# The last 64 queries of a head pair: score products in quarters of TensorE

## Chip, cores and metric

The kernel runs on one core of a Trainium2 chip. The metric is the device time of one execution in microseconds. The kernel before takes 1059.11 us (median of 3 runs, 1058.5 to 1061.32).

## What is computed

Three layers follow one another on 4 batches of 576 tokens: an attention whose probabilities are cut off below the row's maximum less tau, a dense layer with a gate, and a layer of eight experts of which each token uses one. Only the first part of the attention is touched by the change:

```python
def _attn_ref(q, k, v, tau):            # q, k, v: 4 batches, 8 heads, 576 rows, 64 columns
    scale = 1.0 / np.sqrt(q.shape[-1])
    scores = scale * np.matmul(q, k.transpose(0, 1, 3, 2))
    thresh = np.max(scores, axis=-1, keepdims=True) - tau
    scores = np.where(scores >= thresh, scores, -1000000000.0)
    scores = scores - np.max(scores, axis=-1, keepdims=True)
    attn = np.exp(scores)
    attn = attn / (np.sum(attn, axis=-1, keepdims=True) + 1e-09)
    return np.matmul(attn, v)
# then x = attention's rows; g = h * sigmoid(h) with h = x @ w_in; x = g @ w_out;
# then each row through its best expert: gate * relu(x @ w1[e]) @ w2[e]
```

## The kernel before

The attention goes over 16 pairs of heads (4 batches, 4 pairs each). The two heads of a pair lie on the two halves of the 128 partitions: `o.k` has 128 partitions (64 for each head) and 576 columns, `o.q` has 640 columns. The first 512 columns of `o.q` are four chunks of 128 queries. The 64 queries that are left of each head share one chunk, the fifth (`ch == 4`): in its 128 columns the first head's queries stand in columns 0 to 63 of its own 64 partitions, the second head's in columns 64 to 127 of its own, and the host (`layout`) puts zeros elsewhere. One product over all 128 partitions then gives the scores of both heads, the first head's in partitions 0 to 63 of the bank, the second's in 64 to 127.

`score_pe` (L496 and after, the products at L513) makes the scores of a chunk. For chunks 0 to 3 the two heads are two products of 64 rows by 128 columns, in the upper and the lower half of TensorE, into two places of PSUM. The 576 keys are cut: for the first eight pairs (steps below `WIDE`, 72) into four pieces of 144 columns, so that two sets of scores fit side by side, and later into two pieces of 288. Behind the scores come, for each head of a chunk, the maximum on VectorE (`score_max`, L519), the threshold and the exponential on ScalarE (L522, L525), the mask on VectorE (`score_mask`, L540; for chunk 4 it writes `Pm`), transposes on TensorE (L577 and L585, for chunk 4 L593 and L597), copies out of PSUM (L295 on ScalarE, L297 on VectorE), and the products with the values (`values`, L669). Of those the last piece (`j == 4`) has 64 rows for each head:

```python
            for h in range(2):
                rows = slice(None) if j < 4 else HALF[h]
                k = 4 if j == 4 else 5 * h + j
                nc.tensor.matmul(
                    w.av[HALF[h], :nq], lhsT=st.o.vn[rows, k, :], rhs=st.pts[part][rows, k, :],
                    start=(j == 0), stop=(j == 4),
                )
```

Products of the dense layer (L709, L743) are mixed into the attention's from the end of the first batch on. What of them does not fit there, and all of the rest, runs behind the attention (L1117, L1369, L1928, L1932).

The order of the instructions on each engine is written by a planner before the kernel runs. `attend` (L885 and after, the scores' task at L904) makes a task for each step with an engine, an estimated duration, what it waits for and a rank. The planner plays the tasks through and takes, on each engine, the task of the lowest rank among those that can start first or at most its slack later. A TensorE task whose mode (scores, values, or none) differs from the last one's starts `SWITCH`, 0.1 us, later in this play. The score task of a chunk has 1.18 us, whichever chunk it is, rank `s - 0.6`; the maximum has rank `s - 1`, the exponential and the mask `s - 2`, where `s` counts the steps of all pairs. On the chip semaphores alone hold the instructions back; the plan sets their order, not their times.

Of the kernel before, what the change touches and what calls it, by code (L numbers as in the profile page):

```python
# [64 lines left out]
HALF = [slice(0, 64), slice(64, 128)]  # L65
# [195 lines left out]
class Kernel:  # L261
# [234 lines left out]
    def score_pe(self, st, ch, ws, uses):  # L496

        nc = self.nc
        for h, (w, use) in enumerate(zip(ws, uses)):
            w.nm = f"{ch}{h}" + st.nm  # L500
            bank = 3 if use.tag[0] == "B" else 0
            if use.wide:
                at = 512 * bank + 4 * APART * use.slot
                w.S = self.flat[:, at:at + 4 * APART].rearrange("p (a x) -> p a x", x=APART)[:, :, :PIECE]
            else:
                w.S = self.banks[:, bank:bank + 2, :288]
        lhsT = st.o.q[:, 128 * ch:128 * ch + 128]
        n, c = w.S.shape[1:]
        for a in range(n):
            for h, w in enumerate(ws):  # L510

                rows = HALF[h] if ch < 4 else slice(None)
                nc.tensor.matmul(  # L513
                    w.S[:, a], lhsT=lhsT[rows], rhs=st.o.k[rows, c * a:c * a + c], start=True, stop=True
                )

    def score_max(self, w):
# [367 lines left out]
    def attend(self, plan, pair, n, o, x_there):  # L885

        steps = self.steps(pair, o)
        st = steps[0][0]
# [4 lines left out]
        for a, step in enumerate(steps):  # L893
            s = 9.0 * n + a
            _, ch, h = step
            if h == 0:

                pe = []
                for i in range(2 if ch < 4 else 1):
                    w = Obj()  # L900
                    w.use = Token(f"{'AB'[i]}{(9 * n // 2 + n % 2 + (a + 1) // 2) % 2 if s < WIDE else 0}")
                    w.use.wide = s < WIDE
                    pe.append(w)
                score = plan.task(  # L904
                    "pe", 1.18, partial(self.score_pe, st, ch, pe, [w.use for w in pe]),
                    o.there + self.last_s + ([] if s < WIDE else self.last_wide),
                    tuple(w.use for w in pe), (o.k_use, o.q_use), rank=s - 0.6, slack=0.1, mode="scores",
                )
                self.last_s = [score]
                for x in (int(s) - 1, int(s)):  # L910
                    if x in self.held:
                        plan.link(score, self.held.pop(x))
            w = pe[h]
            scores, t = w.use, score
            use = [scores, Token("m"), Token("e")]
            if ch < 4 and h == 0 or ch == 4:
                p_use[ch] = Token("P" if ch < 4 else "Pm")
            mx = plan.task("dve", 0.67, partial(self.score_max, w), (t,), (use[1],), rank=s - 1, slack=0.3)
            t = plan.task("act", 0.84, partial(self.score_exp, w), (mx,), (use[2],), rank=s - 2, slack=0)
            mask = masks[ch, h] = plan.task(  # L920
                "dve", 0.81, partial(self.score_mask, step, w), [t] + list(masks.values())[-1:],
                ((p_use[ch],) if h == 0 else ()) + ((l_use,) if a == 0 else ()), use + [self.more_banks[x] for x in ("wide", "narrow")[s >= WIDE:]], rank=s - 2,
                slack=0.1,
            )
            if s < WIDE:
                self.last_wide = [mask]
            part = min(ch // 2, 1)
            for i, (tag, turn, pieces) in enumerate(self.turns(step)):
                if n == B * H // 2 - 1 and ch > 2:
                    tag = "M"  # L930
                tok = Token(tag)
                give = [self.more_banks["T"]] if tag == "T" else []
                if i and ch < 4:
                    after, us, used = [masks[x, y] for x in (ch - 1, ch) for y in range(2)], 0.24, [p_use[ch - 1], p_use[ch]]
                else:
                    after, us, used = [mask], 0.46 if ch < 4 else 0.3, [p_use[ch]]
                t = plan.task("pe", us, partial(turn, tok), after + (begun[part:part + 1] if i else []), (tok,), used, rank=s + -0.5, slack=0.1)
                for cols, move in pieces:
                    take = ()
                    if part not in part_use:  # L940
                        part_use[part] = Token(f"p{2 * part}")
                        take = (part_use[part],)
                    us = {512: (0.48, 0.6), 256: (0.26, 0.335), 64: (0.11, 0.13)}[cols]
                    x = plan.task(
                        "act", us[0], move, [t] + begun[part:part + 1], take, [tok] + give, rank=s, alt=("dve", us[1])
                    )
                    if take:
                        begun.append(x)
                    moved[part].append(x)
            if ch == 1 and h == 1 or ch == 4:  # L950
                tok = Token("M")
                us, mms, move = self.values(st, part, tok)
                t = plan.task(
                    "pe", 5 * us, partial(run_all, mms), moved[part] + o.v_there + av[-1:],
                    (tok,) if part else (tok, t_use), (part_use[part], o.v_use), rank=s + 1, mode="values",
                )
                av.append(t)
                moved["x"] = moved.get("x", []) + [
                    plan.task("act", 0.31, move, (t,), give=(tok,), rank=s, alt=("dve", 0.36))
                ]  # L960
        s = 9.0 * n + DEN
        dve, pe, act, store, load, mul, out = self.denominators(st)
# [1116 lines left out]
```

## Time and profile before

| | |
|---|---|
| median of 3 runs | 1059.11 us |
| the profiled execution | 1061.68 us |
| its span, first to last instruction | 1059.8 us |
| TensorE busy (matmuls) | 974.7 us, 92% |
| VectorE, ScalarE, GpSimd busy | 709.1, 542.3, 433.4 us |
| mean granted clock of TensorE | 0.965 of 2.4 GHz |

The page gives busy times over the whole span, and then digits for 40 slices of 26.5 us each. Matmuls are pipelined, so one that is listed with 0.29 us may be followed by the next after 0.12 us: the time that a group of matmuls takes is read from its start to the start of the next group, not from the durations. The clock that the profile calls PEclk is the share of 2.4 GHz that TensorE was granted; 0.5 is 1.2 GHz.

### The profile page before, as it was taken

Reading aid. Unit: us, or ns where it says so; the run is one execution under the profiler, and the core shown is the slowest. Engines: PE = TensorE matmul, PEld = TensorE weight load, DVE = VectorE, ACT = ScalarE, POOL = GpSimd, SP = SyncE. Lnnn points to the kernel's source line nnn. Section 1 sums busy time; section 2 is a strip of 40 time slices with the busy share of each in tenths; the row PEclk is TensorE's granted clock in tenths of the full one; section 3 lists DMA queues with packets and bytes.
Section 4 is the critical chain, followed back from the end, with each engine's and each line's share of the span. In section 5 each row is a group of like instructions: output and inputs, shape, how many; then the busy total and the mean of one; then the engine's idle time right before and its main releaser. Section 6 shows DMA issues by size and latency. Waiting matters only on the chain.

```text
span 1059.8 us, 18921 instructions
## 1 busy us (share of the span) xinstructions
PE 974.7 (92%) x6667; PEld 819.9 (77%) x6667; DVE 709.1 (67%) x1674; ACT 542.3 (51%) x1284; POOL 433.4 (41%) x444
## 2 busy tenths in 40 slices
PE   4878888999999999979999999999895999999995
PEld 4555566667667677868898898899784999999994
DVE  5778778877787676488588888888563435445521
ACT  4777766756676465466633333333443444444510
POOL 3565521334352120189645454444534444343210
PEclk7899999999999999999999999999896999999998
DMA  3234312334442221533532111111547555545400
GB/s 129 99 122 132 107 41 87 123 127 150 136 147 87 66 65 53 197 130 116 184 127 66 46 62 51 61 61 42 168 136 198 167 167 156 175 161 175 139 33 15
DMA packets 76401, 119.31 MB, mean 113 GB/s; under 512 B 11668, under 2 KB 38596, under 8 KB 76305
## 3 DMA queue, kind: packets, MB, share of 16 engines
q1 hardware_dynamic: 71857, 107.68, 31.6%
q0 software_dynamic: 4448, 10.40, 3.1%
q8 instruction: 53, 0.87, 0.3%
q14 instruction: 43, 0.35, 0.1%
HBM read 94.04 MB, written 24.82 MB: 112 GB/s over the span
## 4 chain that ended last, share of the span: by engine, by line
PE 40%; issue 6%; POOL 4%; DMA 3%; DVE 1%; ACT 1%; SPq 1%; another core or an unknown queue 0%; POOLq 0%; ACTq 0%; DVEq 0%
PE banks L1117 19%; PE banks L1369 11%; PE banks L1932 6%; PE banks L1928 2%; DMA xg<-x,idx 1%; POOL workwrt L351 1%; POOL workwrt L348 1%; POOL workwrt L352 1%; PE banks L1869 1%; POOL out L1955 1%; PE banks L1979 1%; DMA whrows<-part 1%; DMA idx<-table 0%; DMA when<-moe_expert_emb 0%; DMA part<-po 0%
## 5 line engine op out<-in xcount | busy, mean ns | idle before, releaser
L519 DVE TENSOR_REDUCE m<-banks 128x1 f32<-128x576 f32 x144 | 105.3, 752 | 41.0 <-PE banks L513 34.7
L1094 ACT ACTIVATE whe<-rawe 128x512 fp32r<-128x512 f32 x128 | 77.2, 625 | 92.8 <-PE banks L1932 28.1
L1098 DVE TENSOR_TENSOR wle<-rawe,whe 128x512 fp32r<-128x512 f32 x92 | 63.4, 714 | 88.6 <-ACT whe L1094 88.0
L540 DVE SCALAR_TENSOR_TENSOR P<-banks,m,e 128x576 f32<-128x576 f32 x128 | 103.5, 815 | 27.2 <-ACT e L525 14.4
L525 ACT ACTIVATE e<-banks,m 128x576 f32<-128x576 f32 x144 | 105.5, 733 | 13.4 <-PE banks L513 9.6
L513 PE MATMUL banks<-k,q 64*128 64x144 f32 (+3 forms) x792 | 98.5, 355 | 12.1 <-DVE m L519 4.4
L295 ACT ACTIVATE p<-banks 128x512 f32<-128x512 f32 (+2 forms) x166 | 76.2, 480 | 60.4 <-PE banks L577 49.7
L577 PE MATMUL banks<-ident,P 128*128 128x128 f32 x512 | 84.5, 290 | 19.1 <-ACT p L295 12.6
L577 PEld LDWEIGHTS banks<-ident,P 128*128 128x128 f32 x512 | 58.2, 145 | 47.8 <-ACT p L295 18.4
L669 PE MATMUL banks<-p,v 128*64 128x256 f32 (+3 forms) x640 | 93.6, 430 | 0.0
L513 PEld LDWEIGHTS banks<-k,q 64*128 64x128 f32 (+1 forms) x792 | 69.3, 196 | 28.1 <-issue 6.2
L1337 ACT ACTIVATE t<-banks 128x256 f32<-128x256 f32 x108 | 41.1, 380 | 96.9 <-PE banks L1117 95.3
L1098 POOL TENSOR_TENSOR wle<-rawe,whe 128x512 fp32r<-128x512 f32 x36 | 46.5, 1294 | 98.4 <-ACT whe L1094 78.7
L669 PEld LDWEIGHTS banks<-p,v 128*64 128x64 f32 (+1 forms) x640 | 41.7, 141 | 44.2 <-issue 24.6
L1342 DVE SCALAR_TENSOR_TENSOR g<-t,banks 128x256 f32<-128x256 f32 x108 | 45.0, 417 | 43.8 <-ACT t L1337 38.5
L522 ACT ACTIVATE m<-m,ntau 128x1 f32<-128x1 f32 x144 | 41.9, 291 | 41.0 <-DVE m L519 39.7
L1117 PE MATMUL banks<-xs_6h,wh 128*128 128x256 f32 x216 | 61.8, 286 | 0.0
L1117 PE MATMUL banks<-xs_6h,wl 128*128 128x256 f32 x216 | 61.5, 285 | 0.0
L1117 PE MATMUL banks<-xs_6l,wh 128*128 128x256 f32 x216 | 61.4, 284 | 0.0
L348 POOL TENSOR_TENSOR wa<-wa,wr 128x512 int32<-128x512 int32 x22 | 28.1, 1278 | 63.7 <-DVE wa L343 46.5
L1955 POOL DMA_INDIRECT out<-yr,idx x25 | 25.2, 1007 | 52.1 <-DVE yr L1967 39.2
L709 PE MATMUL banks<-xh,whi 128*128 128x256 f32 x144 | 43.8, 304 | 0.8 <-ACT p L295 0.8
(572 smaller groups left out, 3113.1 us busy)
## 6 DMA issues: line engine op xcount, KB each, us to landing
rawe<-moe_w SPq DMA_DIRECT2D x64, 512.0 KB
wraw<-moe_w_in SPq DMA_DIRECT2D x12, 512.0 KB
wraw<-moe_w_out SPq DMA_DIRECT2D x10, 512.0 KB
q<-q SPq DMA_DIRECT2D x15, 320.0 KB
v<-v SPq DMA_DIRECT2D x16, 288.0 KB
x_dram<-t SPq DMA_DIRECT2D x16, 288.0 KB
part<-po SPq DMA_DIRECT2D x18, 256.0 KB
xc<-x_dram SPq DMA_DIRECT2D x18, 256.0 KB
```

The costliest lines, as they stand in the source:

```text
L295: self.nc.scalar.activation(out=out, in_=src, func=AF.Copy)
L513: nc.tensor.matmul(w.S[:, a], lhsT=lhsT[rows], rhs=st.o.k[rows, c * a:c * a + c], start=True, stop=True)
L519: self.nc.vector.tensor_reduce(out=w.m[:, 0:1], in_=w.S, axis=AX.XY, op=ALU.max, negate=True)
L525: self.nc.scalar.activation(out=w.e, in_=w.S, func=AF.Exp, bias=w.m[:, 0:1])
L540: self.nc.vector.scalar_tensor_tensor(out=P.rearrange("p (a x) -> p a x", a=w.S.shape[1]), in0=w.S, scalar=w.m[:, 1:2], in1=w.e, op0=ALU.i ...
L577: nc.tensor.transpose(T[:, 128 * j:128 * j + 128], st.P[ch][:, c:c + 128], self.ident)
L669: nc.tensor.matmul(w.av[HALF[h], :nq], lhsT=st.o.vn[rows, k, :], rhs=st.pts[part][rows, k, :], start=(j == 0), stop=(j == 4),)
L1094: self.nc.scalar.activation(out=o.tiles[0][:, 2 * a:2 * a + 2], in_=o.raw[:, 2 * a:2 * a + 2], func=AF.Copy)
L1098: self.on[on].tensor_tensor(out=o.tiles[1][:, to], in0=o.raw[:, to], in1=o.tiles[0][:, to].bitcast(F32), op=ALU.subtract)
L1117: self.nc.tensor.matmul(h[:, :n], lhsT=lhs(a, kk), rhs=z[:, kk, :], start=(kk == 0 and i == 0), stop=(kk == 3 and i == 2))
L1369: nc.tensor.matmul(self.banks[:, y_use[d].slot], lhsT=o.gs[z][:, NT * d:NT * d + NT], rhs=wout(f, a), start=(f == fs[0] and i == 0), stop= ...
L1932: nc.tensor.matmul(self.banks[:, y_use[d].slot, :n], lhsT=w2[a][:, 128 * d:128 * d + 128], rhs=o.gs[z], **flags)
```

## The change

For chunk 4 each piece of keys is multiplied in two products, one for each head: the head's own 64 rows and its own 64 columns of the stationary operand, the head's 64 rows of the keys, into the head's half of the partitions. The product with zeros is not made any more; the zeros themselves stay where they were. The planner's estimate for this task goes from 1.18 to 0.65 us. Chunks 0 to 3 are written differently but are the same products.

```diff
--- before.py
+++ after.py
@@ -506,12 +506,18 @@
                 w.S = self.banks[:, bank:bank + 2, :288]
         lhsT = st.o.q[:, 128 * ch:128 * ch + 128]
         n, c = w.S.shape[1:]
+        if ch == 4:
+
+            for a in range(n):
+                for x in HALF:
+                    nc.tensor.matmul(
+                        w.S[x, a], lhsT=lhsT[x, x], rhs=st.o.k[x, c * a:c * a + c], start=True, stop=True
+                    )
+            return
         for a in range(n):
             for h, w in enumerate(ws):
-
-                rows = HALF[h] if ch < 4 else slice(None)
                 nc.tensor.matmul(
-                    w.S[:, a], lhsT=lhsT[rows], rhs=st.o.k[rows, c * a:c * a + c], start=True, stop=True
+                    w.S[:, a], lhsT=lhsT[HALF[h]], rhs=st.o.k[HALF[h], c * a:c * a + c], start=True, stop=True
                 )
 
     def score_max(self, w):
@@ -902,7 +908,7 @@
                     w.use.wide = s < WIDE
                     pe.append(w)
                 score = plan.task(
-                    "pe", 1.18, partial(self.score_pe, st, ch, pe, [w.use for w in pe]),
+                    "pe", 1.18 if ch < 4 else 0.65, partial(self.score_pe, st, ch, pe, [w.use for w in pe]),
                     o.there + self.last_s + ([] if s < WIDE else self.last_wide),
                     tuple(w.use for w in pe), (o.k_use, o.q_use), rank=s - 0.6, slack=0.1, mode="scores",
                 )
```

## Rows read from the trace of the kernel before

**Rows 1.** The page: busy times, and two lines of the 40 slices in tenths.

```profile
PE 974.7 (92%) x6667; PEld 819.9 (77%) x6667; DVE 709.1 (67%) x1674; ACT 542.3 (51%) x1284; POOL 433.4 (41%) x444
...
PE   4878888999999999979999999999895999999995
...
DVE  5778778877787676488588888888563435445521
```

**Rows 2.** Busy times by stretch, us from the start; count; clock, DMA share, GB/s.

```profile
core 0: us, PE busy (x) PEld busy (x) DVE busy (x) ACT busy (x) POOL busy (x), PEclk, DMA share, GB/s
30.00:138.00 108.00, 86.36 (x711) 58.72 (x705) 83.53 (x165) 76.97 (x176) 62.40 (x49) 0.92 0.35 113
138.00:212.00 74.00, 65.88 (x549) 48.16 (x551) 58.23 (x123) 50.38 (x122) 16.32 (x15) 0.98 0.27 88
212.00:420.00 208.00, 204.14 (x1422) 147.59 (x1419) 155.70 (x316) 129.64 (x314) 64.51 (x59) 1.00 0.32 106
420.00:1060.00 640.00, 602.32 (x3895) 551.98 (x3894) 395.77 (x1042) 269.62 (x646) 279.49 (x308) 0.97 0.37 117
```

**Rows 3.** Groups by form, the scores' line: form, count, busy us, mean ns, idle before.

```profile
L513 PE MATMUL banks<-k,q 128*128 128x288 f32 x32 | 9.1, 406 | 0.0
...
L513 PE MATMUL banks<-k,q 128*128 128x144 f32 x56 | 8.6, 298 | 5.1 <-DVE m L519 3.1 <-DVE P L540 1.3 <-ACT e L525 0.6
```

**Rows 4.** TensorE's timeline, chunk 4 at 100.74: start, length, group, count, [idle before].

```profile
100.74 1.15 PE L513 MATMUL banks<-k,q 128*128 128x144 f32 x8
101.73 0.60 PE L577 MATMUL banks<-ident,P 128*128 128x128 f32 x4
```

**Rows 5.** TensorE's timeline, chunk 4 in two pieces, twice, with what follows.

```profile
277.39 1.13 PE L513 MATMUL banks<-k,q 128*128 128x288 f32 x4
278.36 0.60 PE L577 MATMUL banks<-ident,P 128*128 128x128 f32 x4
278.80 0.38 PE L585 MATMUL banks<-ident,P 128*128 128x128 f32 x2
...
216.83 1.13 PE L513 MATMUL banks<-k,q 128*128 128x288 f32 x4
217.90 1.30 PE L669 MATMUL banks<-p,v 128*64 128x320 f32 x8
```

**Rows 6.** Value products of form 64 by 64, then the next group (its weight loads).

```profile
106.25 0.65 PE L669 MATMUL banks<-p,v 64*64 64x256 f32 x4
...
106.83 0.42 PEld L577 LDWEIGHTS banks<-ident,P 128*128 128x128 f32 x4 [0.39 <-issue]
```

**Rows 7.** Timeline, scores of two heads in halves: TensorE's groups, then their weight loads.

```profile
108.17 0.66 PE L577 MATMUL banks<-ident,P 128*128 128x128 f32 x4
108.76 1.25 PE L513 MATMUL banks<-k,q 64*128 64x144 f32 x16
109.94 0.66 PE L577 MATMUL banks<-ident,P 128*128 128x128 f32 x4
110.43 0.27 PE L627 MATMUL banks<-ident,l 128*9 128x128 f32 x1
...
108.76 1.04 PEld L513 LDWEIGHTS banks<-k,q 64*128 64x128 f32 x16 [0.17 <-issue]
```

**Rows 8.** TensorE's timeline, chunk 4 of pair 0, and chunk 4 after idle time.

```profile
26.97 1.28 PE L513 MATMUL banks<-kfirst,qfirst 128*128 128x144 f32 x8
...
126.42 1.25 PE L513 MATMUL banks<-k,q 128*128 128x144 f32 x8 [1.33 <-DVE P L540]
```

**Rows 9.** Timeline of VectorE and of TensorE behind chunk 4 that starts at 77.17.

```profile
78.80 0.76 DVE L519 TENSOR_REDUCE m<-banks 128x1 f32<-128x576 f32 x1 [1.02 <-ACT e L525]
...
80.12 0.66 PE L577 MATMUL banks<-ident,P 128*128 128x128 f32 x4 [1.26 <-ACT p L295]
```

**Rows 10.** A pair's end: TensorE's timeline, then the columns of rows 2 by stretch.

```profile
115.31 0.66 PE L577 MATMUL banks<-ident,P 128*128 128x128 f32 x4 [2.78 <-ACT p L295]
...
116.00:119.30 3.30, 3.30 (x14) 1.53 (x16) 2.08 (x5) 2.11 (x5) 2.71 (x2) 0.50 0.09 25
```

## The prediction

> **What bounds the kernel now.** The page was read first: TensorE is busy for 92% of the span and VectorE for 67%, and in the 40 slices TensorE stands at 9 almost everywhere from the ninth slice on, while in the first eight it is at 7 or 8 and VectorE close behind it [rows 1]. The changed products run from 27 us on [rows 8] through all 16 pairs, the attention, so the next view was the busy time by stretch [rows 2]. Three stretches matter. From 30 to 138 us TensorE works 86.4 of 108 us and VectorE 83.5: neither is full, and the attention's chain from engine to engine sets the pace. From 138 to 212 us TensorE is at 65.9 of 74, because the first products of the dense layer now fill its holes. From 212 to 420 us it is at 204.1 of 208: TensorE is the bound, and whatever is added to its queue there moves the end by as much. What is not done there of the dense layer is done behind 420 us, where TensorE is busy 602 of 640 us, so a delay is not caught up later.
>
> **The change part by part.** For the last 64 queries of each pair (chunk 4) one product of 128 rows by 128 columns becomes two of 64 by 64, one in the upper left and one in the lower right quarter of TensorE. A product of f32 stands in the trace as two matmul instructions. The old group is 8 instructions of 144 columns (four pieces) for the first eight pairs, and 4 of 288 (two pieces) for the last eight; the forms' counts are 56 of the first kind and 8 more for pair 0, and 32 of the second [rows 3, 8]. The new group has twice as many instructions, each over the same number of columns.
>
> *What the old group takes.* In the timeline it starts at 100.74 us and the next group at 101.73, so 0.99 us for 8 instructions, 0.123 each [rows 4]. At the full clock, 2.4 GHz (granted from 212 to 420 us, where rows 2 show 1.00), 144 columns twice are 0.120 us. So the clock was full here too, the instructions follow each other at the rate of the columns, nothing is lost between them, and nothing at the two ends, since the transposes beside it use the whole array too. The narrow form gives the same: 277.39 to 278.36, 0.97 us for four times 0.240 [rows 5].
>
> *What the new group streams.* The nearest row is the last piece of the value products, which has exactly the new form: 64 by 64, the two heads in the same two quarters, into the two halves of the partitions of one bank. Four instructions of 256 columns start at 106.25 us and the next group at 106.83, 0.58 us [rows 6]. One after the other they would need 4 x 0.213 = 0.85; side by side, two pairs, 0.43. So the two quarters do run at once, and each still takes the full time of its columns. For chunk 4 that is 8 x 0.120 = 0.96 us, in the wide form and in the narrow: just what the one big product streams. The zeros beside the queries cost nothing now, because they lie in rows and columns of the array that are passed in the same cycles. The gain in streaming is therefore 0, with +-0.05 us a step for a first load of 64 columns in place of 128.
>
> *What the new group adds.* The 0.58 us are 0.15 over the streaming: a first weight load that nothing covers, and a wait before the next group of another form. The score groups of chunks 0 to 3, which use halves of the array, show the same price: 108.76 to 109.94 is 1.18 us for 0.96 of columns, 0.22 over it [rows 7]. Around it, the four transposes ahead take 0.59 us to the start of the scores and those behind 0.49 [rows 7], where four transposes that nothing interrupts take 278.36 to 278.80, 0.44 [rows 5]. So a group of another form between two groups of the whole array costs 0.10 at its entry (0.59 less the 0.49), 0.15 within and at its exit, and 0.05 at the first load behind it: 0.30 us. Chunk 4 pays this now, and did not before.
>
> The Trainium skill speaks of this pair in "TensorEngine Tiling (Array Packing)", section Gotcha 1: PSUM Pressure: different row tiles, it says, cannot access the same PSUM bank at once, and the two new quarters lie in different row groups and write one bank. By it the pairs would run one after the other, as in the last rival below; rows 6 speak against it, with 0.58 where a sequence takes 0.85.
>
> *The sum over the 16 steps.* I went through the old groups and their neighbours in TensorE's timeline. From 212 to 420 us there are eight: six between groups of the whole array, 0.30 each, and two (as the one at 216.83) followed by value products of another form, which already pay at the exit, 0.15 each [rows 5]: 2.1 us, in a stretch without cover. In the first two stretches there are eight. Five start after an idle TensorE, as that at 126.42 (1.33 us) [rows 8]: the entry is free, and the shorter first load gives some back, so 0.1 each. One lies between transposes (0.30), one, pair 0's, is on the half clock (0.4: most of the 0.30 at twice the length), one follows a group of another form (0.2): 1.4 us in all. Up to 138 us idle time of TensorE stands behind them (as 1.26 us before the transposes at 80.12 [rows 9]) and hides it; if that cover is gone, it costs the 1.0 us of these steps. I take the three steps behind 138 us, where products of the dense layer fill the gaps: 0.4. Sum 2.5 us; bounds 2.1 (all of the early ones hidden) and 3.5 (none), and 0.2 if the switches overlap with the waits of the packed stretch, which no row shows.
>
> *What the plan makes of it.* The program's order on every engine comes from a planner that is told 0.65 us for the step in place of 1.18. It adds 0.1 for a change of mode. By the rows above the step takes about 1.1 to 1.3 us, so the planner, which was 0.2 us too long, is now 0.5 too short. The waits are semaphores, so this changes no result, but it can change which task of VectorE, ScalarE or TensorE is put first from pair 0 on, and each later choice with it. No row shows the new order. I bound its cost by -4.0 and +4.0 us, worked out as rivals, and take 0 for the forecast, since the order before already runs with a wrong duration for this step. No DMA is added or moved by hand; q is still loaded with its zeros.
>
> The profiled execution took 1061.68 us, 1059.8 of it the span; the median is 1059.11, 2.6 lower. The sum gives 1064.2 for an execution like the profiled one, and 1061.6 for the median. About 0.3%, 3.2 us, is what a measurement of this kernel can tell from no change, so the forecast is an unchanged time at its slower edge.
>
> **The rivals.**
> *Planned too short, and late.* VectorE's maximum of chunk 4 is queued behind the step. At 78.80 it starts after 1.02 us of idle [rows 9]. If the planner puts it, 0.5 us too early, ahead of masks that are ready, VectorE stands still and everything queued behind it (masks, copies, the weights' shifts) comes later. Before 212 us VectorE works 142 of 182 us [rows 2], and not all of its idle time lies where it could take this up. Eight steps of 0.5 us are 4.0; with the 2.5 of the switches 1065.6 us. It decides as soon as the maximum is put ahead of a mask that was ready. Against it: the maximum has a later rank than the masks.
> *Planned shorter, and luckily.* The same freedom brings the last mask of a pair forward. At the end of a pair TensorE waits, as 2.78 us until 115.31, and right behind this the clock falls: 0.50 granted, 1.2 GHz, from 116 to 119.3 [rows 10], which is 1.7 us of work lost. The mean of 0.92 from 30 to 138 us [rows 2] is worth 108 x 0.08 = 8.6 us, some five such falls. The planner's 0.53 us at four ends give 2.1, and two to four spared falls 3.4 to 6.8; less 2.5, the time is 3.0 to 6.4 us shorter, about 1054.6. Against it: the wait at 115.31 is for ScalarE's copies, not for chunk 4.
> *Quarters are quicker than the columns.* If the old group's eight loads stood in the open, at 1.04/16 = 0.065 us each (the loads at 108.76 [rows 7]), they would cost 0.52 a step, and the new pairs could cover them: 16 x 0.52 less 3.5 is 4.8 us faster, 1054.3. The 0.99 us of rows 4 leave 0.03 for them, so this hardly lives. It is what the Trainium skill would give, in "TensorE: Matmul & The Clock Gate", Part 3, section The mechanism: weight loads overlap with running matmuls only when the row group differs; the trace disagrees with 0.123 us an instruction.
> *The quarters run one after the other.* Then each step takes 0.96 us more: 16 x 0.96 + 2.5 = 17.9, 1077.0 us.
>
> **How the numbers follow.** Forecast, with the order's effect small: 0.44, between 1059.3 and 1062.6 by its own bounds. Planned too short and late: 0.28. Luckily planned: 0.20. Quicker quarters: 0.04. One after the other: 0.04. Faster by over 0.3% is the third and fourth, 0.24. Within 0.3% is the forecast but for its upper edge, 0.42; slower is that edge, the second and the last, 0.34. The range for 8 in 10 goes from 1055.0 (half of the lucky case) to 1066.5 (nearly all of the late one).
>
> **What would show it.** In the changed profile, groups of form 64 by 64 at the line of the scores should take about 1.1 us from their start to the next group's, in pairs a few ns apart. A start 0.96 us later of the next group would mean a sequence; 0.65 us would mean that the planner's number is true. TensorE's busy share from 212 to 420 us should stay, and the stretch become 2 us longer. If the first stretch moves by more than 1 us, or the number of half-clock windows changes, it is the order and not the products. The prediction is wrong if the order moves more than the switches do.

## The result and the profile after

The changed kernel takes 1072.81 us (median of 4 runs, 1067.39 to 1074.77) against 1060.21 for the kernel before beside it: a ratio of 1.011 with a 95% interval of 1.0067 to 1.0152. The forecast was 1061.6, in a range up to 1066.5; the time lies above it. The profiled execution took 1073.15 us, its span is 1071.5.

The page of the changed kernel, the lines that answer to [rows 1] and the granted clock:

```profile
PE 983.7 (92%) x6763; PEld 818.2 (76%) x6763; DVE 712.2 (66%) x1677; ACT 542.8 (51%) x1284; POOL 429.5 (40%) x441
...
PE   4778788999999999989999999999895999999995
...
DVE  5677766777777767577778888888655444545521
...
PEclk8888888899999999999999999999996999999998
```

The granted clock in the same slices of the kernel before:

```profile
PEclk7899999999999999999999999999896999999998
```

TensorE has 96 matmuls more, 64 in the first eight pairs and 32 in the last, as the change makes them, and 9 us more of busy time. VectorE's digits are lower in several of the first eight slices, and the clock's are 8 there where they were mostly 9. The views by stretch say more. Changed kernel, the stretches of [rows 2] (the columns are the same):

```profile
30.00:138.00 108.00, 84.70 (x694) 54.97 (x692) 81.79 (x162) 73.08 (x166) 59.01 (x46) 0.87 0.36 112
138.00:212.00 74.00, 63.79 (x523) 46.59 (x520) 50.60 (x106) 44.12 (x108) 6.63 (x6) 0.86 0.20 63
212.00:420.00 208.00, 204.50 (x1448) 145.15 (x1448) 154.99 (x313) 130.98 (x320) 76.05 (x70) 1.00 0.35 111
420.00:1075.00 655.00, 614.74 (x4004) 558.13 (x4000) 409.61 (x1067) 278.99 (x663) 277.13 (x306) 0.98 0.36 116
```

In equal times less was done: VectorE did 81.8 us of work instead of 83.5 in the first stretch and 50.6 instead of 58.2 in the second, ScalarE 44.1 instead of 50.4. The clock went from 0.92 to 0.87 and from 0.98 to 0.86. From 212 us on TensorE is as full as before. So the loss begins early, in the stretches where TensorE has idle time.

The next view groups by line over the whole trace: count, shortest, median and longest in ns, and the start of the first and of the last. It gives the last maximum of the attention and the first product of the dense layer, for the kernel before and for the changed one:

```profile
L519 DVE TENSOR_REDUCE m<-banks x144: 697/754/759, 9.3 to 419.2; 128x1 f32<-128x576 f32 x144
L709 PE MATMUL banks<-xh,whi x144: 275/277/581, 138.2 to 428.1; 128*128 128x256 f32 x144
```

```profile
L525 DVE TENSOR_REDUCE m<-banks x144: 740/757/759, 9.3 to 434.6; 128x1 f32<-128x576 f32 x144
L715 PE MATMUL banks<-xh,whi x144: 276/281/388, 156.8 to 443.6; 128*128 128x256 f32 x144
```

The attention's last maximum comes 15.4 us later, and the dense layer, which began early in the sixth pair, begins 18.6 us later. (The lines of the changed file are six higher from the scores on.) Read maximum by maximum, the ninth pair begins at 206.9 us instead of 195.9: 11 of the 15 us are there by then.

The new groups themselves look as expected. Changed kernel, TensorE's timeline, beside [rows 4, 5]:

```profile
103.20 0.38 PE L591 MATMUL banks<-ident,P 128*128 128x128 f32 x2
103.51 1.20 PE L513 MATMUL banks<-k,q 64*64 64x144 f32 x16
104.64 0.66 PE L583 MATMUL banks<-ident,P 128*128 128x128 f32 x4
...
288.78 1.19 PE L513 MATMUL banks<-k,q 64*64 64x288 f32 x8
289.90 0.66 PE L583 MATMUL banks<-ident,P 128*128 128x128 f32 x4
290.39 0.38 PE L591 MATMUL banks<-ident,P 128*128 128x128 f32 x2
```

From start to the next group it is 1.13 us in the wide form and 1.12 in the narrow, where the whole product took 0.99 and 0.97; the four transposes behind take 0.49 instead of 0.44, and the two ahead 0.31 to the start of the group, where they took 0.22 before. The two quarters of a pair start 5 to 8 ns apart. That is the price that was predicted, some 0.3 us a step with the entry, and not 0.8 us a step, which is what 12 us over 16 steps would be.

### The profile page after: what moved, and what is told of

It is laid out like the page before. It is cut to its first block, busy times and chain, and to the rows that moved or that the text cites. A ratio compares the mean times of both kernels' runs of the same rounds, so it can differ in the third digit from the quotient of the medians.

```text
span 1071.5 us, 19082 instructions
## 1 busy us (share of the span) xinstructions
PE 983.7 (92%) x6763; PEld 818.2 (76%) x6763; DVE 712.2 (66%) x1677; ACT 542.8 (51%) x1284; POOL 429.5 (40%) x441
## 4 chain that ended last, share of the span: by engine, by line
PE 41%; issue 6%; DMA 3%; POOL 3%; DVE 1%; ACT 1%; SPq 1%; another core or an unknown queue 0%; POOLq 0%; ACTq 0%; DVEq 0%
PE banks L1123 20%; PE banks L1375 11%; PE banks L1938 6%; PE banks L1934 2%; DVE wle L1104 1%; PE banks L1875 1%; DMA xc<-x_dram 1%; DMA xg<-x,idx 1%; DMA idx<-table 1%; POOL out L1961 1%; POOL workwrt L351 1%; PE banks L1985 1%; POOL workwrt L352 0%; DMA rawe<-moe_w 0%; POOL workwrt L348 0%
## 5 line engine op out<-in xcount | busy, mean ns | idle before, releaser
L1104 DVE TENSOR_TENSOR wle<-rawe,whe 128x512 fp32r<-128x512 f32 x93 | 68.9, 767 | 81.7 <-ACT whe L1100 78.4
L295 ACT ACTIVATE p<-banks 128x512 f32<-128x512 f32 (+2 forms) x172 | 80.3, 483 | 76.6 <-PE banks L583 58.0
L675 PE MATMUL banks<-p,v 128*64 128x256 f32 (+3 forms) x640 | 98.4, 448 | 0.0
L519 PE MATMUL banks<-k,q 64*128 64x144 f32 (+1 forms) x704 | 81.6, 360 | 5.9 <-DVE m L525 3.0
L519 PEld LDWEIGHTS banks<-k,q 64*128 64x128 f32 x704 | 57.4, 199 | 20.0 <-issue 7.7
L740 POOL TENSOR_TENSOR gl<-g,gh 128x256 fp32r<-128x256 f32 x21 | 16.1, 775 | 70.5 <-ACT gh L734 70.5
```

Of the source, the lines that this page charges most:

```text
L295: self.nc.scalar.activation(out=out, in_=src, func=AF.Copy)
L519: nc.tensor.matmul(w.S[:, a], lhsT=lhsT[HALF[h]], rhs=st.o.k[HALF[h], c * a:c * a + c], start=True, stop=True)
L675: nc.tensor.matmul(w.av[HALF[h], :nq], lhsT=st.o.vn[rows, k, :], rhs=st.pts[part][rows, k, :], start=(j == 0), stop=(j == 4),)
L1104: self.on[on].tensor_tensor(out=o.tiles[1][:, to], in0=o.raw[:, to], in1=o.tiles[0][:, to].bitcast(F32), op=ALU.subtract)
```

## The experiments

### Products and order, one at a time

The change has two parts: the products, and the number that the planner is told. The first kernel has the new products and the old number, the second the old product and the new number.

```diff
# e1_quarters_old_order, against the changed kernel
-                    "pe", 1.18 if ch < 4 else 0.65, partial(self.score_pe, ...
+                    "pe", 1.18, partial(self.score_pe, ...
# e2_whole_new_order, against the kernel before
-                    "pe", 1.18, partial(self.score_pe, ...
+                    "pe", 1.18 if ch < 4 else 0.65, partial(self.score_pe, ...
```

> Quarter products as in the changed kernel, but the planner is told 1.18 us for the step again; every engine then has the instructions of the kernel before in the same order, with chunk 4's products split. Theory O (the new order makes the loss): the time of the kernel before plus the 2.5 us of the changes of form that were predicted, about 1062.7 us (1060.5 to 1064). Theory P (the quarter products themselves make it): as the changed kernel, about 1072 us.

> The one product with zeros of the kernel before, but the planner is told 0.65 us; every engine has the order of the changed kernel. Theory O: nearly the changed kernel's time, less the 2.5 us, about 1070 us. Theory P: the time of the kernel before, about 1060 us.

Put beside the two kernels that the case began with, this is a table of two by two (median, number of runs, ratio to the kernel before and its interval; the changed kernel's entry is the one above, measured beside 1060.21 us):

| | order of 1.18 us | order of 0.65 us |
|---|---|---|
| one product with zeros | 1060.62 (23), 1 | 1074.18 (4), 1.0127 [1.0099, 1.0156] |
| two products in quarters | 1060.33 (12), 0.9994 [0.9977, 1.0012] | 1072.81 (4), 1.011 [1.0067, 1.0152] |

The order makes the whole loss, with either form of the product, and the quarters make no difference that can be measured, with either order. Theory P falls. What e1 also shows is less than theory O expected: 2.5 us for the changes of form would be a ratio of 1.0024, and the interval ends at 1.0012.

From 20 to 220 us the busy times of the kernel before, of e1, of e2 and of the changed kernel are, in this order:

```profile
20.00:220.00 200.00, 167.42 (x1348) 118.07 (x1348) 155.45 (x312) 139.20 (x323) 89.36 (x72) 0.93 0.30 97
```

```profile
20.00:220.00 200.00, 167.29 (x1406) 116.23 (x1408) 153.46 (x311) 138.22 (x321) 90.83 (x72) 0.93 0.30 95
```

```profile
20.00:220.00 200.00, 160.93 (x1256) 114.29 (x1256) 146.69 (x293) 130.04 (x304) 77.66 (x62) 0.88 0.29 90
```

```profile
20.00:220.00 200.00, 164.23 (x1326) 114.13 (x1328) 145.73 (x294) 130.55 (x304) 78.15 (x62) 0.86 0.28 89
```

The third engine's time, VectorE's, tells roughly how far a kernel has come. It falls by 9 us with the order and by 2 with the products; the clock follows the order too, 0.88 and 0.86 against 0.93.

### Where the order matters

```diff
# e3_065_first_pairs, against the changed kernel; e4 has s >= WIDE
-                    "pe", 1.18 if ch < 4 else 0.65, partial(self.score_pe, ...
+                    "pe", 0.65 if ch == 4 and s < WIDE else 1.18, partial(self.score_pe, ...
```

> Quarter products everywhere, 0.65 us told for the first eight pairs alone, 1.18 for the others. If the loss is made by the order in the first 212 us (theory O1): about 1072 us. If it is made by the order in the last eight pairs (theory O2): about 1063 us. Theory P: 1072 us.

> Quarter products everywhere, 0.65 us told for the last eight pairs alone; the first eight have the old order. Theory O1: about 1063 us, as the old order with quarters. Theory O2: about 1072 us. Theory P: 1072 us.

e3 took 1073.24 us (ratio 1.0112 [1.0082, 1.0142]) and e4 1061.19 (1.0022 [0.9995, 1.0049]). So it is theory O1: the number told for the first eight pairs makes the loss. Told for the last eight alone, it also rewrites their order, at no cost that can be measured. In the traces, too, the loss is there by the ninth pair: from its first maximum to the attention's last one the changed kernel takes 227.7 us, e3 227.7 and e1, in the old order, 227.1. (The kernel before takes 223.3 us; the products and a stretch at half clock make that difference, as is said below.)

### The start of the dense layer

The largest visible difference of the two orders is when the dense layer starts to fill TensorE's holes. The next pair of experiments moves that start: later in the old order, earlier in the new one.

```diff
# h1_old_order_late_dense, against the kernel before
-                    () if t else tuple(use.values()), (x_use,), rank=rank,
+                    () if t else tuple(use.values()), (x_use,), rank=rank, held=blk == kk == 0,
                 )
+                if blk == kk == 0:
+                    self.first_moe = getattr(self, "first_moe", []) + [t]
...
                 self.last_s = [score]
+                if n == 5 and ch == 4:
+                    for x in self.first_moe:
+                        plan.link(score, x)
# h2_new_order_early_dense, against the changed kernel
-        rank = 1000.0 + blk
+        rank = 1000.0 + blk if blk else 38.0
```

> The kernel before, whole product and 1.18 us, but the first block of the dense layer may start only behind chunk 4 of the sixth pair, as in the changed kernel (156.8 us there, 138.2 before); the pairs up to then keep the old order. Theory M (the late start of the dense layer, which leaves TensorE's holes open, makes the larger part of the loss, the 7 us that come behind the fifth pair): about 1067 us. If not: about 1061 us.

> The changed kernel, but the first block of the dense layer has a rank of 38 in the plan in place of 1000, so that it starts at the end of the fifth pair, as in the kernel before; the pairs ahead of it keep the new order. Theory M: the 7 us come back, about 1066 us. If not: about 1073 us.

h1 took 1064.16 us, 1.0024 [0.9999, 1.005]; h2 1068.27, 1.0083 [1.0051, 1.0116]. The late start costs the old order about 2.5 us, hardly beyond what can be told, not the 7 of theory M. h2 lies 4.5 us below the changed kernel's median, but the intervals of the two ratios overlap, and h2 is not the clean opposite of h1: with a rank of 38 the whole first block goes ahead of the sixth pair's tasks, not its start alone. At 160 us 24 products of the line shown below have begun, where the kernel before has 8, and the sixth pair takes 37.4 us from its first maximum to the next pair's, where the changed kernel takes 24.0. So the start of the dense layer is a part of the loss, about a fifth by h1; from h2 its share can't be told. In h1's trace the first product of the dense layer is at 155.0 us and the attention's last maximum at 428.1, 8.9 us later than before; that execution, the slowest of h1's ten, took 1067.16 us, 5.5 more than the profiled one before:

```profile
L519 DVE TENSOR_REDUCE m<-banks x144: 697/754/759, 9.3 to 428.1; 128x1 f32<-128x576 f32 x144
...
L709 PE MATMUL banks<-xh,whi x144: 276/278/562, 155.0 to 437.0; 128*128 128x256 f32 x144
```

### The half clock

From 20 to 220 us the changed kernel's profile has 55 us at half clock, that of the kernel before 28: the stretches at the ends of the pairs are longer. To tell the clock from the waits that go with it, TensorE was given more to do in its waiting time.

```diff
# f1_new_order_fillers (changed kernel) and f2_old_order_fillers (kernel before)
+    def filler(self, n):
+        for _ in range(3 if n < 7 else 0):
+            self.nc.tensor.matmul(self.flat[:, 1376:1504], lhsT=self.ident, rhs=self.ident, start=True, stop=True)
# called behind the transposes of chunk 4 (twice a pair), of two chunks' shared columns (twice), of st.l
# f4_new_order_ahead (changed kernel) and f5_old_order_ahead (kernel before)
+    def filler(self, T, n):
+        for _ in range(4 if n < 5 else 0):
+            self.nc.tensor.matmul(T[:, 384:512], lhsT=self.ident, rhs=self.ident, start=True, stop=True)
# called ahead of the transposes of chunk 0 and of chunk 4, with their own bank T
```

> The changed kernel, its order untouched, with three more products of 128 columns (0.21 us each at the full clock) into an unused strip of PSUM behind four places of each of the first seven pairs where TensorE soon waits: both sets of chunk 4's transposes, the transposes that two chunks share, and that of the denominators. They compute nothing that is used. Theory K (the half clock at the ends of the pairs makes the loss: 55 us at half clock up to 220 us against 28 before): the windows of half clock go, about 1062 us or less. Theory W (the waits of the new order make it, whatever the clock): 1073 us or a little more, as the added work delays what is behind it.

> The kernel before with the same added products at the same places. Theory K: its own windows of half clock, 28 us up to 220 us, go too, at half their length in work up to 10 us: about 1053 us. Theory W: 1061 us or a little more.

f1 took 1081.52 us (1.0192 [1.0146, 1.0238]) and f2 1066.26 (1.0058 [1.0035, 1.0081]): both slower than without the fillers. But they tell little, because the strip lies in a bank that ScalarE reads, and the added products waited for it. TensorE's timeline of f1:

```profile
69.72 0.94 PE L526 MATMUL banks<-ident 128*128 128x128 f32 x6 [1.50 <-ACT e L536]
```

The second form has no such wait; it uses the bank that the transposes take anyway.

> The changed kernel, its order untouched, with four more products of 128 columns (0.21 us each at the full clock) ahead of the transposes of each pair's first chunk and of chunk 4, for the first five pairs, into the bank that these transposes then overwrite. They wait for the bank alone, and the transposes behind them for the mask, so they fill time in which TensorE waited. They compute nothing that is used. Theory K (the half clock itself costs): fewer windows of half clock, and about 1066 us. Theory W (the pairs are as long as the chain of waits makes them, at either clock): 1072 to 1075 us.

> The kernel before with the same added products at the same places. Theory K: about 1056 us. Theory W: 1060 to 1063 us.

f4 took 1080.03 us (1.0177 [1.0135, 1.022]), f5 1061.44 (1.0011 [0.9987, 1.0035]). Busy times from 20 to 220 us, f4 and then f5:

```profile
20.00:220.00 200.00, 170.28 (x1438) 124.52 (x1438) 144.96 (x286) 128.33 (x297) 74.48 (x59) 0.92 0.27 87
```

```profile
20.00:220.00 200.00, 173.14 (x1469) 127.75 (x1469) 153.12 (x306) 137.70 (x317) 87.29 (x71) 0.98 0.30 95
```

The clock does come back: 0.92 in f4, where e2 had 0.88 and the changed kernel 0.86, and 0.98 in f5. The value products at a pair's end show it. First the changed kernel, then f4:

```profile
67.54 1.08 PE L583 MATMUL banks<-ident,P 128*128 128x128 f32 x4 [3.81 <-DVE P L546]
68.56 5.03 PE L675 MATMUL banks<-p,v 128*64 128x320 f32 x20
```

```profile
62.86 1.16 PE L526 MATMUL banks<-ident 128*128 128x128 f32 x8
...
67.96 3.06 PE L683 MATMUL banks<-p,v 128*64 128x320 f32 x20
```

TensorE waited 3.81 us there and then ran the 20 products in 5.03 us; with work in the gap they take 3.06. But VectorE's work, 144.96 us, is no further than in the changed kernel (145.73). The fillers bring their own cost: four groups a pair of some 1.1 us each (62.86 to 63.95), 22 us over five pairs. In the old order these 22 us cost nothing that can be measured, in the new one 7. Theory K's times fell in none of the four runs; f5 fits theory W, f4 fits neither, and the two effects cannot be parted by these runs. What can be said is that getting the clock back by added work does not get the time back.

Two traces on record say more on what the half clock costs by itself. The changed kernel and e3 have the same instructions in the same order on every engine up to 291 us. From the second pair's first maximum to the ninth's the changed kernel takes 171.0 us, with 48 us at half clock, and e3 174.4 us, with 58: 10 us more at half clock go with 3.3 us. e1, in the old order, takes 162.7 us with 20 us at half clock, and has as many of the dense layer's first products behind it by then, 16. At the rate of the first two, 27 us less at half clock would be worth 9 us, and the two orders differ by 8.3. By this estimate, from one execution of each kernel, the half clock may be most of the loss up to the ninth pair. It isn't shown: no run held the clock without adding work.

### Is it the wrong number, or another order

The 0.65 us are too short by half a microsecond. If that were the reason, a number nearer to the truth should bring the time back. Two more numbers, both with quarters:

```diff
# n1_quarters_told_095; n2_quarters_told_13 has 1.3
-                    "pe", 1.18 if ch < 4 else 0.65, partial(self.score_pe, ...
+                    "pe", 1.18 if ch < 4 else 0.95, partial(self.score_pe, ...
```

> Quarter products, the planner told 0.95 us, closer to the 1.13 us that they take. Theory S (the loss comes from telling too short a time and grows with the error): 1061 to 1065 us. Theory L (any other number gives another order, good or bad, whatever its error; what counts is where the dense layer starts, here behind the sixth pair's chunk 4): 1066 to 1072 us.

> Quarter products, the planner told 1.3 us, a little longer than they take. Theory S: no loss, 1060 to 1063 us. Theory L: the dense layer starts behind the sixth pair's chunk 4 here too, so 1066 to 1072 us.

n1 took 1066.54 us (1.007 [1.0044, 1.0096]) and n2 1070.7 (1.0084 [1.005, 1.0119]). With quarters, whose step takes 1.13 us from start to the next group, the numbers 0.65, 0.95, 1.18 and 1.3 give 1072.8, 1066.5, 1060.3 and 1070.7 us. An error of 0.05 gives the best time, but one of 0.17, on the long side, is nearly as bad as one of 0.48 on the short side. Theory S alone falls with n2. The second half of theory L, that the start of the dense layer is what counts, isn't borne out either: it starts at 148.7 us in n1, 156.6 in n2 and 156.8 in the changed kernel, but also at 155.0 in h1, which takes 1064.2 us.

Each other number gives another order, 0.65 and 0.95 from the first pair on, 1.3 from the third, and of the four orders the old one is the fastest, by 5 to 13 us. Four orders are few; that every other order would be slower is not shown. Nor do the others lose in one place: against e1, n2's trace is 3.0 us late at the ninth pair's first maximum, 5.2 at the attention's last one and 10.5 at the end. n1's profiled execution, 1061.19 us, was the fastest of its nine and does not show where the others lose.

### Does TensorE's time in the attention count

The prediction called the first stretch partly covered and the stretch from 212 us on bound by TensorE. In the order of e1, chunk 4's products were made three times over, once in the last eight pairs alone and once in the first eight alone:

```diff
# r1_threefold_last, against e1; r3_threefold_first has "3 if wide else 1"
+            wide = uses[0].wide
-            for a in range(n):
+            for a in [a for _ in range(1 if wide else 3) for a in range(n)]:
```

> Quarter products in the old order, but in the last eight pairs chunk 4's products are made three times over into the same place: 1.94 us more for TensorE in each of eight steps, 15.5 us in all, in the stretch that was called bound by TensorE. If TensorE's time there reaches the end, as predicted: 1060.3 + 15.5 = 1076 us. If waits behind 420 us take up what comes late (theory A): clearly less, 1068 us or below.

> The same in the first eight pairs alone, 15.5 us more for TensorE between 27 and 200 us. By the prediction the first five steps are hidden by idle time and the last three are not, 5.8 us: about 1066 us. If the chain of waits passes through these products: up to 1076 us.

r1 took 1074.09 us, 1.011 [1.008, 1.0141], and r3 1076.18, 1.013 [1.0097, 1.0164]. Against the 1060.3 us of e1 the 15.5 us of added work came out as 13.8 in the last eight pairs and as 15.9 in the first eight; by the ratios to the kernel before beside them it is 11.7 us (8.5 to 15.0) and 13.8 (10.3 to 17.4). In the last eight most of it or all counts, as predicted. In the first eight it does too, where 5.8 were expected. Busy times from 20 to 220 us of r3:

```profile
20.00:220.00 200.00, 167.25 (x1555) 120.57 (x1556) 141.07 (x284) 127.30 (x293) 78.77 (x62) 0.93 0.27 88
```

TensorE is busy for 167.25 of 200 us, as in e1 with 167.29, although it has 149 matmuls more in them. Its idle time stays the same and everything else comes later: VectorE's work falls from 153.46 to 141.07 us, and the ninth pair's first maximum comes at 212.6 us instead of 197.1, later by all of the 15.5 us.

## Why the prediction was wrong

**The order.** The step that failed is the value taken for the planner's new number: 0, between bounds of -4.0 and +4.0 us. e2 measures it: 13.6 us (1074.18 less 1060.62), over three times the bound. The upper bound was eight times the planner's error of 0.5 us, as if a wrong duration could cost no more than its error at each place; the lower one, -4.0, does not follow from its rival, whose gains add up to 5.5 to 8.9 us. But the number does not shift the plan, it makes another one. From between 30 and 40 us on, in the first two pairs, other tasks are first on TensorE, VectorE, ScalarE and GpSimd, the dense layer starts 18.6 us later, and choices that have nothing to do with chunk 4 come out otherwise. The reason given for 0, that the old order already ran with a wrong duration, does not carry: that one order is fast with a number 0.2 us too long says nothing of what another number brings, and 1.3, 0.17 us too long for the quarters, brings 1070.7 us (n2).

**The rivals.** "Planned too short, and late" had the right sign and the right place (the order of the first eight pairs, e3), but its mechanism, VectorE held up by half a microsecond behind each chunk 4, was sized at 4.0 us and is not what the traces show. The groups of VectorE's maxima from 20 to 220 us, in the kernel before and in the changed one, have behind the second bar the idle time before them and what ended it:

```profile
L519 DVE TENSOR_REDUCE m<-banks 128x1 f32<-128x576 f32 x77 | 57.1, 752 | 19.7 <-PE banks L513 16.3 <-ACT e L525 3.0
```

```profile
L525 DVE TENSOR_REDUCE m<-banks 128x1 f32<-128x576 f32 x73 | 54.3, 754 | 24.4 <-PE banks L519 19.1 <-ACT e L531 3.5 <-PE banks L513 0.9
```

Before the maxima there are 24.4 us of idle instead of 19.7. In the changed kernel 19.1 are ended by the scores of the other chunks (L519) and 0.9 by chunk 4's (L513); in e1, where the two lines are apart as well, it is 14.0 and 0.9. What grew is the wait for chunks 0 to 3. "Quarters are quicker" and "one after the other" are refuted by the 1.13 us of the new group and by e1.

**The products.** Their price in the trace was right: 1.13 and 1.12 us predicted as 1.11, with 0.05 behind and 0.10 ahead. In the last eight pairs of e1, whose instructions match those before one by one, the lag behind the kernel before grows from 1.2 us at the end of the first eight to 5.0 at 421 us, 1.6 of it in one step near 269 us, where that execution fell to half clock and the other did not; 2.2 remain, where the sum for these eight was 2.1. What failed is that this reaches the end. e1's last instruction is at 1059.6 us, the other's at 1059.8, and over all runs the difference is -0.6 us, between -2.4 and +1.3, where 2.5 was the sum. Where the 2.5 us go is not settled. In these two profiles the lag falls to 3.0 us by 560, to 0.8 near 752 and to -0.2 near 803 us; at 522 and at the two later places the execution of the kernel before spends more time at half clock than that of e1. One pair of profiles cannot tell a gain from such a difference. One reading was off without weight: pair 0's group [rows 8] starts only 0.3 us before the half clock ends, so its 0.4 us were too much.

**The cover.** Up to 138 us the added time was held to be hidden by TensorE's idle time, 1.26 us behind one step [rows 9]. r3 shows that 1.94 us a step are not hidden there, not even in part: the idle time of an engine in a chain of waits moves along with the work in front of it. Whether the 0.1 to 0.3 us a step of the change itself are hidden it does not show. In e1, e4 and r1, whose instructions are the same through the first eight pairs, the ninth begins 1.2, 0.0 and 0.3 us later than before, where the sum was 0.4 with the cover and 1.4 without it. The last eight pairs were judged rightly, with nearly no idle time [rows 2] and 13.8 of 15.5 us counted.

**What stays open.** The order of the first eight pairs makes the loss; the late dense layer is about 2.5 us of it by h1. The rest, in the first five pairs (5.3 us by the sixth pair's first maximum, 138.9 against 133.6) and in the three behind them, was not traced to single choices. The time at half clock, 48 us against 20 up to the ninth pair, goes with a loss of this size, but its share was not parted from that of the waits by a run.

## What to carry to other kernels

When a number that a planner reads is changed together with the code, the two are two changes: cost them apart, give the order a range as wide as other orders have been seen to spread, here 13 us of 1060, and measure each without the other. Two small products in opposite quarters of the array streamed no faster here than one product over the whole array with zeros, and cost changes of form beside: 1.13 us against 0.99 a group. Idle time of an engine is cover only if the work behind it does not wait for the work in front: adding a known amount there and looking at the end tells, for an amount of that size.

## What the runs showed of the hardware

Two quarters in different rows and columns of the array wrote two halves of the partitions of one bank at the same time: 16 instructions of 144 columns in 1.13 us, of which 0.96 is the streaming of eight pairs. Such a group between groups of the whole array cost 0.30 us (0.10 ahead, 0.15 within, 0.05 at the next group's first load).

The granted clock fell to half in gaps of TensorE at pairs' ends, in the changed kernel at 65.7 us in the gap from 63.7 to 67.5, and the 20 products behind it took 5.03 us instead of 3.06. That the granted clock from 20 to 220 us rose to 0.98 in f5, against 0.93, by added work of 22 us without a gain in time was not expected.
